# Attention on one NeuronCore: the shifted-V moves issued by SyncE and GpSimd instead of SyncE and ScalarE

## The chip, the cores and the metric

The kernel runs on one core of one Trainium2 chip. Its engines are TensorE (PE; its weight loads are shown apart as PEld), VectorE (DVE), ScalarE (ACT), GpSimd (POOL) and SyncE (SP). SP, ACT and POOL can each issue DMA transfers; all transfers of the core run on the same 16 DMA engines. The metric is the time of one execution on the device in microseconds. Runs of this kernel before the change took 480.32, 483.03 and 484.62 us, median 483.03.

## What is computed

A sequence of 2048 tokens with 512 channels passes through four layers: state-space convolution, attention, convolution, attention, each with a layer norm before it and a residual around it. The change concerns the attention, which looks at eight earlier tokens with a step of two:

```python
def _B_ref(x, wqkv, wo):
    H = 32; Dh = D // H              # D = 512, so Dh = 16
    W, dil = 8, 2
    qkv = ...                        # x @ wqkv, as (3, B, H, S, Dh)
    q, k, v = qkv[0], qkv[1], qkv[2]
    idx = arange(S)[:, None] - (arange(W) * dil)[None, :]
    mask = idx >= 0
    idx_c = where(mask, idx, 0).reshape(-1)
    kg = k[:, :, idx_c, :].reshape(B, H, S, W, Dh)
    vg = v[:, :, idx_c, :].reshape(B, H, S, W, Dh)
    logits = einsum("bhsd,bhswd->bhsw", q, kg) * Dh ** -0.5
    attn = softmax(where(mask, logits, -1e9), axis=-1)
    o = einsum("bhsw,bhswd->bhsd", attn, vg)
    return o.transpose(...).reshape(B, S, D) @ wo
```

## The kernel before

**Stages.** First the convolution's kernel is generated (about 117 us), then come the convolution layer, attention layer 0 (from about 180 to 300 us), the second convolution and attention layer 1 (from about 355 us to the end). Token 16 p + j lies in partition p, column j, so a step of two tokens is a step of two columns, and a step past column 0 goes to the partition above.

**Attention** (`b_layer`). A layer is split into blocks, named in the lists `ORDERS` (line 691): `K0`..`K3` and `Q00`..`Q31` are the projections of keys and queries (line 843 on PE, cast by ACT at 845); `L..` the logits (products `prodqk` on DVE at 871, summed over a head by PE at 885, cast by ACT at 888 into `Lsb`); `S..` the softmax (maxima on DVE at 943, 949 and 951; subtraction on PE at 961 and 962 in layer 0, on DVE at 954 in layer 1; exponentials on ACT at 964 or 955; the sum on PE at 969, its reciprocal by two ACT instructions at 971 and 972, into `sm_rdb`; the scaling on DVE at 973); `V0` and `V1` the two halves of V; `P..` the products with V (`prodpv` on DVE at 992, summed by PE at 999, cast by ACT at 1011); `R..` the output rows (lines 1022 to 1036) and, in layer 0, the norm and the first stage of the next convolution.

**V and its shifted copy.** Each half of V (`fp` 0 or 1, 256 channels) lies in a table `V2` of 128 partitions x 2 x 22 rows x 256. PE projects it in eight pieces (line 899) and ACT casts them into rows 14 to 21 (line 906). The rows below, 0 to 13, hold the same values shifted by one partition or by 64; `v_shift` (line 911) fills them with nine DMA transfers inside SBUF, each of which waits for all eight casts. The first four fill rows 6 to 13 (64, 48, 15 and 1 partitions with 8 KB each, the last with 4 KB), the other five rows 0 to 5 (48, 15, 48 and 15 partitions with 6 KB each, and two with 3 KB). Every product of a half waits for all nine.

**Who issues them.** In half 0 moves 1, 4 and 7 go through ACT's queue and the other six through SP's, in half 1 all nine through SP's. The transfer is issued by the engine in its own sequence, between its other instructions:

```python
act = fp == 0 and k % 3 == 1
o = plan.add("ACT" if act else "SP", 0.65, lambda move=move, act=act: move(nc.scalar if act else nc.sync), need)
```

**What sets the order.** `Plan` (line 621) is a list scheduler that runs while the kernel is built. Each operation has an engine, a cost in us, the operations that it follows and the buffers that it takes. `Plan.run` repeatedly picks the operation that could start earliest by these costs and emits it, a tie going to the lower priority number and then to the order of blocks in `ORDERS`. The emission order is the order in which each engine works, whatever the durations on the chip are. A move costs 0.65 us on its issuing engine; its transfer is an operation of a made-up engine `dma`, which takes one transfer after another at 230 GB/s, and a product may follow 2 us after that. ACT's clock in the plan thus holds three times 0.65 us per layer for moves.

**Other users of the queues.** SP's queue also carries the loads `Kt` of the convolution (line 262; those for the second convolution stand behind V1's moves of layer 0), the zeros of the `V2` tables (737 and 738) and two of the four output stores (142). ACT issues the other two stores. POOL loads five small constants at the start and sets small tables; its last instructions of the kernel's work are at 117 us.

Of the kernel before, what the change touches and what calls it, by code (L numbers as in the profile page):

```python
# [11 lines left out]
ACT = mybir.ActivationFunctionType  # L12
# [694 lines left out]
def b_layer(nc, tc, C, Xg, Ng, Wt, last_layer, y_rows, es_y):  # L707
# [5 lines left out]
    with ExitStack() as es:  # L713
# [43 lines left out]
                m.Z = pool("a_z", 1, es_z).tile([128, NGR, 128], BF, name="Z")  # L757

        pr = PRIO[last_layer]
        plan = Plan({"-": 0.0, "PE": 0.0, "DVE": 0.5, "ACT": 0.5, "SP": 0.0} | {"dma": 0.0})  # L760
        y_sums, x_sums = ((),) * 4, ((0, 1, 2, 3), (0, 1, 2, 3), (0, 1), ())
        PA, PL, PO, PQ, PV = ("psA", 4), ("psL", 2), ("psO", 2), ("prodqk", 5), ("prodpv", 8)
        got = {}
# [147 lines left out]
        def v_shift(fp):  # L911

            moves = [(64, 0, 64, 6, 14, 8, 0), (1, 64, 48, 6, 14, 8, 0), (49, 112, 15, 6, 14, 8, 0), (0, 127, 1, 6, 14, 8, 1)]
            moves += [(64 * h + d, 64 * h + d - 1, n, 0, 16, 6, 0) for h in range(2) for d, n in ((1, 48), (49, 15))]
            moves += [(0, 63, 2, 0, 16, 6, 1)]
            need = [got["V", fp, c, jp] for c in range(2) for jp in range(4)]
            for k, (d, f, n, rd, rs, nr, wrap) in enumerate(moves):
                def move(eng, d=d, f=f, n=n, rd=rd, rs=rs, nr=nr, wrap=wrap):
                    T = m.V2[fp]
                    step = 64 if n == 2 else 1  # L920
                    lanes = [slice(x, x + (n - 1) * step + 1, step) for x in (d, f)]
                    cd, cs = (slice(1, 2), slice(0, 1)) if wrap else (slice(0, 2), slice(0, 2))
                    eng.dma_start(T[lanes[0], cd, rd:rd + nr, :], T[lanes[1], cs, rs:rs + nr, :])
                act = fp == 0 and k % 3 == 1
                o = plan.add("ACT" if act else "SP", 0.65, lambda move=move, act=act: move(nc.scalar if act else nc.sync), need)
                o = plan.add("dma", V_MOVE_US + n * nr * 1e-3 * 512 * (1 if wrap else 2) / V_RATE, lambda: None, [o])
                got["V2", fp].append(plan.add("-", 0.0, lambda: None, [o]))
                got["V2", fp][-1]["lag"] = V_LAND
# [163 lines left out]
        def v_half(fp):  # L1092
            for c in range(2):
                for jp in range(4):
                    proj_v(fp, c, jp)
            v_shift(fp)
# [36 lines left out]
def kernel(  # L1133
# [62 lines left out]
    for layer in range(2):  # L1196
        y_rows, es_y = a_layer(nc, tc, C, Xg, Ng, kt_dram, load_w, Z, es_z)
        Z, es_z = b_layer(nc, tc, C, Xg, Ng, Wt, layer == 1, y_rows, es_y)
# [31 lines left out]
```

## Time and profile before

| | |
|---|---|
| median of three runs | 483.03 us |
| the profiled execution: its own time | 480.45 us |
| the profiled execution: span from first to last instruction | 478.7 us |
| mean granted clock of TensorE | 0.949 |
| DMA packets, data moved | 37873, 45.55 MB |
| DMA data through SP's queue / ACT's queue / POOL's queue | 41.77 / 2.91 / 0.13 MB |
| moves of V: SP issues, duration of one (min, median, max) | 30; 0.559, 0.910, 2.767 us |
| moves of V: ACT issues, duration of one (min, median, max) | 6; 0.677, 1.680, 2.551 us |
| from issue to landing of a move (min, median, max) | 5.8, 7.6, 9.1 us |

The profile is one execution. Busy time of an engine is time in its instructions; an issue of a DMA is not counted as busy and is shown on a queue (SPq, ACTq), with the time for which it holds the engine's sequence. A line of the timeline gives start, duration, engine, line of the code, operation, tiles and, in brackets, how long the engine had been idle before and what ended that; "issue" there means that nothing the profile shows was waited for. The chain of waits is followed back from the last instruction to whatever released each step.

The moves were issued at 221.8 to 229.2 us (layer 0, V0), 244.3 to 254.6 (layer 0, V1), 410.1 to 418.6 (layer 1, V0) and 426.4 to 436.3 (layer 1, V1); the landings recorded last came at 234.2, 257.0, 422.1 and 440.3 us.

### The profile page before, as it was taken

The numbers are of one execution on the slowest core, as the hardware profiler recorded it, in microseconds if no ns is written. First come the engines' busy times: TensorE is split into PE (matmuls) and PEld (weight loads), VectorE is DVE, ScalarE is ACT, GpSimd is POOL, SyncE is SP. The second block draws the span as 40 slices with busy tenths as digits, with TensorE's granted clock in tenths as the row PEclk, the third lists the DMA queues.
The fourth block names the chain that finished last, engine by engine and source line by source line (L and its number), as shares of the span: only waits on it lengthen the run. The fifth ranks groups of instructions, "written<-read, shape, count | busy, mean of one in ns | idle before, by whom it ended". The sixth has DMA issues, their size and how long they took to land.

```text
span 478.7 us, 11624 instructions
## 1 busy us (share of the span) xinstructions
PE 400.8 (84%) x4764; PEld 263.1 (55%) x4764; DVE 411.1 (86%) x848; ACT 334.4 (70%) x568; POOL 5.7 (1%) x26
## 2 busy tenths in 40 slices
PE   2006788979998979999898899879989999888996
PEld 1002358456446754577676665357744567776662
DVE  4899999998349878879899999989878899899990
ACT  5987997974667977854675269969978657652354
POOL 3000000001000000000000000000000000000000
PEclk9999995979999999999999699999999999996699
DMA  8930001424669990003444105029700000645022
GB/s 253 423 117 0 2 0 17 92 56 88 162 155 265 260 286 11 2 2 79 78 94 107 46 1 178 1 60 269 202 1 2 2 3 1 122 91 98 1 88 90
DMA packets 37873, 45.55 MB, mean 95 GB/s; under 512 B 27924, under 2 KB 29204, under 8 KB 36924
## 3 DMA queue, kind: packets, MB, share of 16 engines
q1 hardware_dynamic: 34898, 41.77, 32.8%
q10 hardware_dynamic: 2762, 2.91, 2.6%
q8 instruction: 37, 0.61, 0.5%
q0 software_dynamic: 160, 0.13, 0.1%
q14 instruction: 16, 0.13, 0.1%
HBM read 30.55 MB, written 6.29 MB: 77 GB/s over the span
## 4 chain that ended last, share of the span: by engine, by line
PE 55%; ACT 16%; DVE 15%; DMA 5%; issue 4%; SPq 3%; ACTq 1%; DVEq 0%
PE ps_qk L843 9%; PE ps_v L899 6%; PE po L999 5%; PE psg L453 5%; PE ps_o L1024 4%; PE Lp L885 3%; ACT n_junk L173 3%; ACT xc L289 3%; DVE prodqk L871 3%; DMA Kt<-kt_scratch 3%; PE psk L430 3%; DVE prodpv L992 2%; PE xp L212 2%; ACT Vtab L477 2%; PE vp L279 2%
## 5 line engine op out<-in xcount | busy, mean ns | idle before, releaser
L871 DVE TENSOR_TENSOR prodqk<-qT,N 128x1024 bf16<-128x1024 bf16 (+3 forms) x176 | 83.9, 539 | 4.4 <-ACT N L845 2.2
L992 DVE TENSOR_TENSOR prodpv<-V,Lsb 128x1024 bf16<-128x1024 bf16 (+1 forms) x160 | 81.9, 577 | 1.3 <-DMA V<-V 0.7
L843 PE MATMUL ps_qk<-xnT,wqk 128*128 128x512 bf16 x256 | 61.1, 379 | 2.7 <-ACT xnT L830 2.2
L999 PE MATMUL po<-halves,prodpv 128*128 128x64 bf16 x1024 | 51.5, 208 | 5.3 <-DVE prodpv L992 2.9
L999 PEld LDWEIGHTS <-prodpv 128*128 128x128 bf16 x1024 | 43.1, 107 | 16.9 <-DVE prodpv L992 10.5
L475 PE MATMUL psadd<-cp,sb_ident 128*128 128x512 bf16 (+3 forms) x48 | 18.4, 384 | 33.0 <-DVE cp L334 30.2
L296 DVE TENSOR_TENSOR pab<-xc,Kt 128x2048 bf16<-128x2048 bf16 x32 | 39.1, 1223 | 7.0 <-ACT xc L289 3.6
L453 PE MATMUL psg<-G,rows 128*128 128x512 bf16 x160 | 38.8, 399 | 1.3 <-DMA rows<-KT 1.3
L1011 ACT CAST oT<-po 128x512 bf16<-128x512 f32 x32 | 17.5, 588 | 30.4 <-PE po L999 30.3
L843 PEld LDWEIGHTS <-wqk 128*128 128x128 bf16 x256 | 23.3, 97 | 25.3 <-issue 1.1
L289 ACT CAST xc<-xp 128x1024 bf16<-128x1024 f32 x32 | 32.7, 1021 | 5.7 <-PE xp L212 5.7
L281 ACT CAST VT<-vp 128x1024 bf16<-128x1024 f32 x32 | 32.5, 1020 | 4.4 <-PE vp L279 4.4
L279 PE MATMUL vp<-sb_IC,pab 128*128 128x128 bf16 x512 | 33.7, 219 | 2.1 <-DVE pab L296 2.1
L334 DVE TENSOR_TENSOR cp<-Vtab,L 128x896 bf16<-128x896 bf16 (+6 forms) x64 | 34.1, 594 | 0.7 <-PE psadd L476 0.4
L885 PEld LDWEIGHTS <-prodqk 128*128 128x128 bf16 x1024 | 30.6, 96 | 5.8 <-DVE prodqk L871 1.6
L279 PEld LDWEIGHTS <-pab 128*128 128x128 bf16 x512 | 29.9, 98 | 3.6 <-DVE pab L296 2.6
L885 PE MATMUL Lp<-sb_bones,prodqk 128*128 128x8 bf16 x1024 | 31.0, 166 | 1.0 <-DVE prodqk L871 0.9
L899 PE MATMUL ps_v<-wv,xnT 128*128 128x256 bf16 x256 | 31.4, 272 | 0.5 <-ACT qT L845 0.5
L334 DVE TENSOR_TENSOR cp<-Utab,L 128x256 bf16<-128x256 bf16 (+4 forms) x60 | 29.2, 544 | 0.9 <-PE psadd L476 0.8
L797 DVE BATCH_NORM_STATS2 ln_stats<-X 128x6 f32<-128x512 bf16 x38 | 24.3, 679 | 4.9 <-ACT X L1071 4.6
L430 PE MATMUL psk<-Utab,Vtab 128*64 128x42 bf16 x512 | 24.1, 203 | 4.9 <-ACT KT L438 2.8
L453 PEld LDWEIGHTS <-rows 128*128 128x128 bf16 x160 | 16.1, 102 | 21.8 <-issue 3.8
(160 smaller groups left out, 765.7 us busy)
## 6 DMA issues: line engine op xcount, KB each, us to landing
Kt<-kt_scratch SPq DMA_DIRECT2D x64, 256.0 KB, 5.1
G<-c_G SPq DMA_DIRECT2D x4, 1280.0 KB, 16.6
kt_scratch<-ks SPq DMA_DIRECT2D x16, 256.0 KB, 2.6
X<-in_A_u_dram SPq DMA_DIRECT2D x4, 512.0 KB
F1Tsb<-c_F1T SPq DMA_DIRECT2D x2, 1024.0 KB, 8.5
V<-V SPq DMA_DIRECT2D x4, 512.0 KB
V<-V SPq DMA_DIRECT2D x6, 288.0 KB
F1sb<-c_F SPq DMA_DIRECT2D x1, 1024.0 KB
```

The lines of the kernel that those rows point to most:

```text
L279: nc.tensor.matmul(vp[:, g, :], pab[:, g, ab, :], IC[:, ab, :], start=(ab == 0), stop=(ab == 1))
L289: nc.scalar.copy(xc[:].rearrange("q g o l -> q (g o l)"), xp)
L296: last = nc.vector.tensor_tensor(pab[:], xc[:].to_broadcast([128, 8, 2, 128]), kts[cg][:], ALU.mult)
L334: nc.vector.tensor_tensor(prod[i, r].rearrange("n (h e t) -> n h e t", h=hn, t=2), a(r), m[:, i].unsqueeze(2).to_broadcast([128, hn, e, 2] ...
L430: nc.tensor.matmul(ps[:, hl, 0:2 * NU], V[:, h, r, :, :].rearrange("n v t -> n (v t)"), U[:, h, r, 0:NU, :].rearrange("n u t -> n (u t)"), ...
L453: mms = [nc.tensor.matmul(ps[:, hf, :], rows[:, t, :], Gt[b][:, t, hf * 512:(hf + 1) * 512], start=(t == 0), stop=(t == 4)) for t in range ...
L843: nc.tensor.matmul(t.ps[:], wqk[:, ct, f0:f0 + 128], x_group(g)[:, :, ct], start=(ct == 0), stop=(ct == 3))
L871: nc.vector.tensor_tensor(b.pr[:, u:u + 2 * n, 1 - a, :], cols(qT[i][:, ja * 128:(ja + n) * 128]), cols(kT[i][:, k0:k0 + n * 128]), ALU.mult)
L885: nc.tensor.matmul(t.Lp[:, w, u % 2, u // 2, :], b.pr[:, u].rearrange("f a q -> f (a q)"), bones[:], start=False, stop=(w == W // 2 - 1 an ...
L899: nc.tensor.matmul(t.ps[:, jj, :], tokens(ct, jp * 2 + jj, c), wv[:, ct, fp * 256:(fp + 1) * 256], start=(jj + ct == 0), stop=(jj == 1 and ...
L992: nc.vector.tensor_tensor(t.p2[:, 0:nj, :].rearrange("p j (d h) -> p j d h", d=DH), m.V2[i // 2][:, c, r0:r0 + nj, f0:f0 + 128].rearrange( ...
L999: nc.tensor.matmul(po[jj // k][:, jj % k, c, :], t.p2[:, jj, :], fold, start=(c == 0 and w == 0 and jj % k == 0), stop=(c == 1 and w == W ...
```

## The change

Every second move (1, 3, 5 and 7) is issued by POOL, the others (0, 2, 4, 6 and 8) by SP, in both halves of both layers. ACT issues none. The planner gets a clock for POOL and charges it 0.65 us for each of its moves. Nothing is changed in what is transferred, or in what waits for it.

```diff
@@ -757,7 +757,7 @@
         pr = PRIO[last_layer]
-        plan = Plan({"-": 0.0, "PE": 0.0, "DVE": 0.5, "ACT": 0.5, "SP": 0.0} | {"dma": 0.0})
+        plan = Plan({"-": 0.0, "PE": 0.0, "DVE": 0.5, "ACT": 0.5, "SP": 0.0, "POOL": 0.0, "dma": 0.0})
@@ -921,8 +921,8 @@
                     eng.dma_start(T[lanes[0], cd, rd:rd + nr, :], T[lanes[1], cs, rs:rs + nr, :])
-                act = fp == 0 and k % 3 == 1
-                o = plan.add("ACT" if act else "SP", 0.65, lambda move=move, act=act: move(nc.scalar if act else nc.sync), need)
+                second = k % 2 == 1
+                o = plan.add("POOL" if second else "SP", 0.65, lambda move=move, second=second: move(nc.gpsimd if second else nc.sync), need)
                 o = plan.add("dma", V_MOVE_US + n * nr * 1e-3 * 512 * (1 if wrap else 2) / V_RATE, lambda: None, [o])
```

## The prediction

> **What bounds the kernel.** I read the busy times first, then the busy time in stretches around the four groups of moves (V0 and V1 in each attention layer), then the chain of waits and the timelines there.
>
> ```profile
> PE 400.8 (84%) x4764; PEld 263.1 (55%) x4764; DVE 411.1 (86%) x848; ACT 334.4 (70%) x568; POOL 5.7 (1%) x26
> ...
> 222.00:228.00 6.00, 6.00 (x102) 3.97 (x99) 4.35 (x10) 2.16 (x6) 0.00 (x0) 1.00 0.82 173
> 228.00:236.00 8.00, 6.48 (x58) 4.37 (x57) 6.48 (x15) 6.24 (x13) 0.00 (x0) 1.00 0.57 102
> 236.00:250.00 14.00, 14.00 (x250) 11.19 (x247) 14.00 (x27) 9.06 (x19) 0.00 (x0) 1.00 0.33 67
> ...
> 410.00:416.00 6.00, 5.37 (x124) 4.14 (x122) 4.85 (x14) 2.82 (x7) 0.00 (x0) 1.00 0.78 155
> 416.00:426.00 10.00, 9.39 (x137) 8.54 (x137) 9.71 (x23) 7.99 (x20) 0.00 (x0) 1.00 0.49 94
> 426.00:436.00 10.00, 7.96 (x152) 6.19 (x149) 10.00 (x19) 3.02 (x6) 0.00 (x0) 0.83 0.77 152
> ```
>
> After the stretch come PE, PEld, DVE, ACT and POOL busy, the clock, the DMA share and GB/s. VectorE (DVE) and TensorE (PE) bound the attention together: right behind V0's moves of the first layer both are busy 14.00 of 14.00 us. Only where the moves run is either idle, with the DMA engines near 0.8 busy. What the change can win lies in that idle time. ScalarE's (ACT's) timeline there, first layer:
>
> ```profile
> 222.52 0.68 ACTq L923 DMA_DIRECT2D V<-V  x1
> 222.66 0.61 ACT L888 CAST Lsb<-Lp 128x512 bf16<-128x512 f32 x1
> 223.77 0.37 ACT L971 ACTIVATE den<-den 128x256 f32<-128x256 f32 x1 [0.51 <-PE den L969]
> 223.78 1.33 ACTq L923 DMA_DIRECT2D V<-V  x1
> 225.24 0.39 ACT L972 ACTIVATE sm_rdb<-den 128x256 bf16<-128x256 f32 x1 [1.10 <-issue]
> 225.26 2.55 ACTq L923 DMA_DIRECT2D V<-V  x1
> 227.86 1.07 ACT L845 CAST qT<-ps_qk 128x512 bf16<-128x512 f32 x2 [2.23 <-issue]
> ...
> 229.45 0.43 DVE L943 TENSOR_TENSOR sm_m<-Lsb 128x512 bf16<-128x512 bf16 x1 [3.11 <-ACT Lsb L888]
> ```
>
> Three issues hold ACT's queue for 4.56 us; two casts behind the third start 2.23 us late, the logits' cast (line 888) behind them is late too, and DVE waits 3.11 us for it. Last, the chain of waits at V1 of the second layer:
>
> ```profile
> 425.80 0.59 ACT V L906
> ...
> 427.11 2.32 SPq L923
> ...
> 434.83 5.47 DMA V<-V
> ...
> 440.43 0.70 DVE prodpv L992
> ```
>
> All nine moves go through SyncE (SP) from 426.41; the last data land at 440.30, 13.9 us after the evict, and DVE waits 0.67 us.
>
> **The change part by part.** Over both layers ACT's moves go from 6 to 0, SP's from 30 to 20, GpSimd's (POOL's) from 0 to 16. In V0, moves 1 and 7 go from ACT to POOL, 3 and 5 from SP to POOL, 4 from ACT to SP; in V1, moves 1, 3, 5, 7 from SP to POOL. No byte is saved: each half still moves 1782 KB (127 lanes x 8 KB, 126 lanes x 6 KB, two wraps).
>
> *Moves off ACT, first layer.* ACT gains 4.56 us, but that is not the gain of the kernel. DVE has work until 226.35, so its wait shrinks by at most the 3.1 us from there to 229.45. Behind it come 6 us of DVE work, then the first prodpv at 235.52, which needs V0; V0's last landing in the trace is at 234.16. So DVE can come forward only 1.36 us before it waits for the moves instead. PE is idle 1.52 us in 228 to 236 and full before and behind, which allows about the same. Gain: 1.4 us, if V0 lands when it does now.
>
> *Moves off ACT, second layer.* The issues hold ACT 5.15 us; the reciprocal (sm_rdb) waits 1.22 us behind the last, and DVE 1.28 us for it. V0 lands at 422.08, the first prodpv starts at 423.42: slack 1.34. PE has 0.63 + 0.61 us idle from 410 to 426. Gain: 1.2 us.
>
> *Moves off SP.* V0, on two queues now, lands 12.3 and 12.0 us after the first issue; V1, on one, 12.6 (244.34 to 256.96) and 13.9. A second queue thus buys 0 to 1.9 us, because the transfers fill most of it: 1782 KB in 10.5 us is 170 GB/s. I take 12.3 for all four halves. V1 of the second layer then lands 1.6 us earlier and its 0.67 us wait goes. V1 of the first is first read by DVE at 262.4, covered by 5.4 us. Behind SP's V1 moves there stand the next layer's Kt loads, from 254.66; they may start some 4 us earlier and share the DMA engines with V1's tail, inside that cover. In the second layer only the output stores at 457 stand behind. Nothing for that.
>
> *Moves onto POOL.* POOL has nothing between 118 and 478 us, so no one is queued behind its four moves and their wait for V's evicts. The trace has five small POOL loads, from the start:
>
> ```profile
> Drow<-in_A_Dskip_dram POOLq DMA_DIRECT2D x1, 1.0 KB, 4.6
> ...
> sb_IC<-c_IC POOLq DMA_DIRECT2D x1, 64.0 KB, 4.1
> ...
> rows<-KT SPq DMA_DIRECT2D x24, 20.0 KB, 1.9
> ```
>
> One issue takes 0.51 to 0.68 us, 128 rows included; a half's four take 2.0 to 2.7 us. A landing is 2.7 us later than SP's small ones (4.6 against 1.9). The wait on POOL is the four moves one after the other, 2.7 + 4.6 = 7.3 us plus their 568 KB beside SP's 1214 KB; with the engines shared evenly that is 2 x 568 / 170 = 6.7 us, so they are down by about 10 of the 12.3 us. SP's last move still ends the half: I take no change, with bounds of -2 (the engines at the 16 x 4096 B / 319 ns = 205 GB/s that the median packet gives) and +5 us (rival A).
>
> *DVE beside POOL.* The windows of the moves hold only TENSOR_TENSOR on DVE. No descriptor writing overlaps DVE in the trace. Bounds: 0, and 16 x 0.53 = 8.5 us if each issue stops a DVE that is full. The nearest row is POOL's 128x512 memset at 116.45: 0.53 us beside DVE's TENSOR_SCALARs, 0.55 us alone. I take 0.
>
> The Trainium skill ("SBUF — State Buffer", section "SBUF: two separate sides") speaks against the change: GpSimd writes a DMA's descriptors through a port pair shared with VectorE, and a VectorE instruction in a two-port mode shuts it out. Its section "Who interferes with whom" exempts tensor_tensor, which it says, as inferred, takes only the read side. No run here shows either. By the page's 3.1 us for a shut-out DMA, four make 12.4 us and V would land at 17.0 us instead of 12.3; as an estimate that costs 3 x 4.7 - 3.3 = 11 us.
>
> *The planner's order.* The planner charged ACT 0.65 us for each of three moves per layer and now charges nothing, so instructions are emitted in another order behind V0. PE is full there, and what ACT does next waits for PE, so I expect few swaps. Nearest price of a bad one: DVE's 1.69 us wait for sm_rdb at 286.3. Bounds -2 to +3; I take 0.4 per layer, 0.8 in all.
>
> *Sum.* -1.4 - 1.2 - 0.7 + 0.8 = -2.5 us. The profiled execution took 480.45 us (span 478.7 plus 1.75 around it), so 478.0 for such a one; the median of the three runs is 2.6 us higher, so 483.0 - 2.5 = 480.5.
>
> **Rivals.**
>
> *A, slower: POOL writes descriptors only while DVE is idle.* It decides once the fourth issue ends later than 12.3 - 4.6 = 7.7 us behind the evict, that is at 1.9 us an issue instead of 0.53. A half needs 4 x 0.53 = 2.1 us of DVE idle. First layer, V0: the 3.1 us gap gives it, nothing lost. Second layer, V0: only 1.3 us are there; DVE reaches prodpv at 422.1, stands still, POOL does the remaining 0.8 us and the data land 4.6 us later, 427.5 against 423.4: +4.1. V1: DVE has no gap before 439.8, so 2.1 + 4.6 puts prodpv at 446.5 against 440.4: +6.1. With -1.4 and the order's 0.8: +9.6, 492.6. If instead POOL stops DVE, 8.5 - 2.5 = +6.0, 489.0. For it: DVE is 97 to 100% busy at these places, and no DMA of POOL has run beside it. Against it: the memset. The skill's exemption stands against it too.
>
> *B, order:* another sequence behind V0 makes new waits of 1.7 us, two per layer: 4 x 1.7 - 3.3 = +3.5, 486.5; or it packs DVE better: DVE's idle time from the first issue to the last landing of all four halves is 51.1 - 45.85 = 5.3 us, and with the 1.69 us at 286.3 gone as well the time is 476.0 at best. For it: every wait behind V0 hangs on this order. Against: PE full.
>
> *C, no gain:* V lands later by about what ACT gives back (x = 1.1 us at three places): 483. For it: POOL's landings of 4.6 us. It differs from the forecast by less than can be measured.
>
> **How the numbers follow.** Forecast 0.40, C 0.15, A 0.23, B slower 0.12, B faster 0.10. The forecast's own range is 477.5 to 483.5. About 1% (4.8 us) is what a measurement of this kernel can tell from no change; its three runs span 4.3. Faster than 478.2: B faster and a little of the forecast, 0.15. Slower than 487.9: A and a tail of B, 0.28. Within: 0.57. The range leaves out A's far end and the last of B faster: 476 to 490.
>
> **What would show it.** Right: no ACT gap "<-issue" behind V0; line 943's wait gone or turned into prodpv waiting about 1.7 us for V in the first layer; POOL's L923 rows near 0.5 us; V landing 12 us behind its evict everywhere. Wrong: POOL rows of 2 us or more, prodpv waiting for V several us at 422 or 440 (A); DVE's prodqk of 128x1024 above 0.69 us (DVE stopped by POOL); or waits on lines other than these behind V0 (B).

## The result, and the profile after

The changed kernel took 478.79 us (median of 21 runs, 476.10 to 481.92) beside 481.37 us before it (21 runs, 478.81 to 485.61): ratio 0.9948, 95% interval 0.9927 to 0.9968, that is -2.5 us. The same kernel, timed again in a later set, gave 477.61 us beside 481.67 us, ratio 0.9918 (0.9895 to 0.9940). It is a little faster, by 0.5 and 0.8 per cent in the two sets. The forecast gain of 2.5 us came in the first set, and about 4.0 us came in the second. The forecast time of 480.5 us was 1.7 us too high: it was counted from a median of three runs, 483.0 us, where 21 runs put the kernel before at 481.4.

The two profiled spans hide this: 478.4 us after, 478.7 before. The attention simply starts later in the profile of after. The zeros of its first `V2` table, which the change does not touch, are written at 192.23 us instead of 190.16; over the profiles of this study that moment lies anywhere between 188.6 and 193.2 us. From 160 to 190 us the mean granted clock was 1.00 in the profile of before and 0.94 in that of after; whether this is the whole shift is not shown. So each layer is read from its own first move; over the two stretches compared here the granted clock is 0.93 and 0.87 in both profiles. From there to the layer's last `prodpv` the first layer takes 74.77 us instead of 76.23, and from there to the last cast of `X` the second takes 63.23 us instead of 64.62: together -2.85 us.

The busy times, and the windows around the moves (those of the first layer put 2 us later than before's), with PE, PEld, DVE, ACT and POOL busy, the clock, the DMA share and GB/s:

```profile
PE 396.1 (83%) x4728; PEld 260.3 (54%) x4764; DVE 410.6 (86%) x848; ACT 334.8 (70%) x568; POOL 14.6 (3%) x42
```

```profile
224.00:230.00 6.00, 6.00 (x103) 4.05 (x102) 4.91 (x12) 4.24 (x9) 2.22 (x4) 1.00 0.86 198
230.00:238.00 8.00, 7.95 (x127) 6.24 (x127) 7.97 (x17) 5.66 (x11) 0.00 (x0) 1.00 0.48 85
238.00:252.00 14.00, 14.00 (x206) 10.48 (x203) 14.00 (x27) 9.26 (x19) 2.23 (x4) 1.00 0.46 95
...
410.00:416.00 6.00, 6.00 (x139) 4.93 (x137) 6.00 (x18) 4.88 (x11) 2.23 (x4) 1.00 0.70 168
416.00:426.00 10.00, 9.47 (x169) 8.68 (x168) 9.44 (x22) 6.66 (x13) 0.35 (x1) 1.00 0.51 88
426.00:436.00 10.00, 7.86 (x129) 6.42 (x126) 10.00 (x21) 3.16 (x7) 1.88 (x4) 0.62 0.93 183
```

POOL's 14.6 us and 42 instructions include its 16 issues, which the profile counts as busy, unlike those of SP and ACT. In the first two windows DVE was busy 4.35 + 6.48 us of 14; now it is 4.91 + 7.97, and PE has no hole left (6.00 + 7.95). At 410 DVE is full where it had lost 1.15 us. POOL's four issues for V1 of the first layer and those for V0 of the second lie inside windows in which DVE and PE are both full (238 to 252, 410 to 416); in the window of V0 of the first layer DVE is busy 4.91 of 6 us. ACT's timeline behind V0 of the first layer:

```profile
223.76 1.09 ACT L964 ACTIVATE Lsb<-ps_sub 128x512 bf16<-128x512 f32 x2
224.73 0.61 ACT L888 CAST Lsb<-Lp 128x512 bf16<-128x512 f32 x1
225.41 0.58 ACT L845 CAST qT<-ps_qk 128x512 bf16<-128x512 f32 x1
225.90 0.37 ACT L971 ACTIVATE den<-den 128x256 f32<-128x256 f32 x1
226.30 0.38 ACT L972 ACTIVATE sm_rdb<-den 128x256 bf16<-128x256 f32 x1
226.81 0.58 ACT L845 CAST qT<-ps_qk 128x512 bf16<-128x512 f32 x1
```

No issue and no bracket with "<-issue" is left; the 1.10 and 2.23 us gaps are gone, and the instructions follow one another. DVE's timeline, first layer and then second:

```profile
229.50 0.63 DVE L871 TENSOR_TENSOR prodqk<-qT,N 128x512 bf16<-128x512 bf16 x2 [1.09 <-ACT N L845]
230.04 0.42 DVE L943 TENSOR_TENSOR sm_m<-Lsb 128x512 bf16<-128x512 bf16 x1
...
235.59 1.90 DVE L992 TENSOR_TENSOR prodpv<-V,Lsb 128x1024 bf16<-128x1024 bf16 x3
...
422.19 0.69 DVE L992 TENSOR_TENSOR prodpv<-V,Lsb 128x1024 bf16<-128x1024 bf16 x1
423.44 1.29 DVE L992 TENSOR_TENSOR prodpv<-V,Lsb 128x1024 bf16<-128x1024 bf16 x2 [0.56 <-DMA V<-V]
...
439.02 4.91 DVE L992 TENSOR_TENSOR prodpv<-V,Lsb 128x1024 bf16<-128x1024 bf16 x8
```

In the first layer line 943's wait of 3.11 us has become one of 1.09 us, for another cast of ACT that PE's projections hold up. In the second layer the wait of 0.67 us for V1 (at 440) is gone, and a wait of 0.56 us for V0 has come in its place at 423. The chain of waits runs through V0's moves there, where it ran through V1's before:

```profile
410.10 0.59 ACT V L906
410.71 0.66 SPq L923
411.37 0.05 issue
411.42 2.87 SPq L923
...
415.32 8.00 DMA V<-V
...
423.44 1.29 DVE prodpv L992 x2
```

POOL's timeline, with the idle time before each group, and the groups of line 923 (duration in ns, min/median/max; first and last start):

```profile
224.16 2.22 POOL L923 DMA_DIRECT2D V<-V  x4 [105.08 <-ACT V L906]
244.78 2.23 POOL L923 DMA_DIRECT2D V<-V  x4 [18.40 <-ACT V L906]
410.98 2.23 POOL L923 DMA_DIRECT2D V<-V  x4 [163.97 <-DVE Lsb L954]
```

```profile
L923 SPq DMA_DIRECT2D V<-V x20: 655/1192/2867, 223.9 to 430.8; - x20
...
L923 POOL DMA_DIRECT2D V<-V x16: 497/574/587, 224.2 to 427.3; - x16
```

POOL takes 0.50 to 0.59 us for an issue, all four right behind the evict. The halves are down 11.7, 12.0, 12.6 and 11.9 us behind their first issue (12.3, 12.6, 12.0 and 13.9 before).

### The profile page after: what moved, and what is told of

Same layout as the page of the kernel before. It is cut to its first block, busy times and chain, and to the rows that moved or that the text cites. A ratio compares the mean times of both kernels' runs of the same rounds, so it can differ in the third digit from the quotient of the medians.

```text
span 478.4 us, 11628 instructions
## 1 busy us (share of the span) xinstructions
PE 396.1 (83%) x4728; PEld 260.3 (54%) x4764; DVE 410.6 (86%) x848; ACT 334.8 (70%) x568; POOL 14.6 (3%) x42
## 4 chain that ended last, share of the span: by engine, by line
PE 55%; DVE 17%; ACT 17%; issue 4%; DMA 3%; SPq 2%; ACTq 0%; DVEq 0%
PE ps_qk L843 9%; PE psg L453 6%; DVE prodpv L992 6%; PE po L999 5%; PE ps_o L1024 5%; ACT xc L289 4%; PE pt L200 3%; PE Lp L885 3%; PE ps_v L899 3%; DVE prodqk L871 3%; ACT n_junk L173 3%; PE vp L279 3%; PE xp L212 3%; PE psk L430 2%; ACT Vtab L477 2%
## 5 line engine op out<-in xcount | busy, mean ns | idle before, releaser
L453 PE MATMUL psg<-G,rows 128*128 128x512 bf16 x156 | 40.1, 414 | 5.0 <-DMA klast<-KT 4.5
L845 ACT CAST N<-ps_qk 128x512 bf16<-128x512 f32 x32 | 18.8, 586 | 14.2 <-PE ps_qk L843 14.1
```

The costliest lines, as they stand in the source:

```text
L453: mms = [nc.tensor.matmul(ps[:, hf, :], rows[:, t, :], Gt[b][:, t, hf * 512:(hf + 1) * 512], start=(t == 0), stop=(t == 4)) for t in range ...
```

## The experiments

Two things change at once: the queues, and the planner's charges, from which the order of the instructions follows. The theory: the gain is ACT rid of its six issues; which queue takes them, and the new order, are worth little. Rivals: the second queue brings it (V down earlier), POOL's descriptor writing costs DVE or waits for it, or the order decides. All versions but the probe differ in the two lines of the change alone. The first diff is against the changed kernel, and those behind it show only what stands in place of its two added lines. Where one of them shows the queue alone, the line with the planner's charge is that of the first version for the new order and that of the second for the old order.

**The new order with the old queues.** The planner charges POOL and SP, while ACT and SP issue as before.

```diff
-                second = k % 2 == 1
-                o = plan.add("POOL" if second else "SP", 0.65, lambda move=move, second=second: move(nc.gpsimd if second else nc.sync), need)
+                queue = nc.scalar if fp == 0 and k % 3 == 1 else nc.sync
+                o = plan.add("POOL" if k % 2 else "SP", 0.65, lambda move=move, queue=queue: move(queue), need)
```

> PE and DVE run in the changed kernel's order, but the moves go through the queues of before (ACT issues 1, 4 and 7 of V0). Queue theory (the gain is ACT's and SP's queue time): no gain, between 0 and +1 us of 481.4, and ACT again shows idle time ended by 'issue' behind V0; since ACT's three issues now stand close together they may hold it 4 to 6 us in one piece. Order theory (the gain comes from the new order): -2.6 us, the same as the changed kernel.

Measured: 486.51 us, ratio 1.0112 (1.0065 to 1.0160), +5.2 us: a miss of the theory, which priced the order by itself. ACT's timeline of this version, first layer and then second:

```profile
222.35 3.08 ACTq L923 DMA_DIRECT2D V<-V  x1
222.77 0.38 ACT L971 ACTIVATE den<-den 128x256 f32<-128x256 f32 x1
225.55 0.38 ACT L972 ACTIVATE sm_rdb<-den 128x256 bf16<-128x256 f32 x1 [2.40 <-issue]
...
411.84 3.19 ACTq L923 DMA_DIRECT2D V<-V  x1
```

A planner that does not know of ACT's issues packs ACT's work as if that time were free, and single issues hold ACT for 3.08 and 3.19 us. The first `prodpv` comes 15.2 us behind the first move in both layers, against 11.7 and 11.5 in the changed kernel with the same order. So the issues on ACT cost more than the 2.0 us that the change gave back at that place, and the old charges had hidden a part of them.

**The new queues with the old order.**

```diff
+                queue = nc.gpsimd if k % 2 else nc.sync
+                o = plan.add("ACT" if fp == 0 and k % 3 == 1 else "SP", 0.65, lambda move=move, queue=queue: move(queue), need)
```

> PE, DVE and the rest of ACT run in the order of before; the moves go through SP and POOL as changed. Queue theory: -2.6 to -3.3 us (the forecast's -1.4 - 1.2 - 0.7, with or without its 0.8 for the order). In layer 0 the 3.1 us wait of line 943 falls by about 2 us or more, in layer 1 the 1.3 us wait for sm_rdb and the 0.67 us wait for V1 go. Order theory: 0 us.

Measured: 477.93 us, ratio 0.9939 (0.9912 to 0.9965). The whole gain is there without the new order.

**All nine moves on SP, new order, then old order.** ACT is free, and there is no second queue.

```diff
+                queue = nc.sync
```

> The changed kernel's order, all 36 moves on SP. If freeing ACT is what counts and POOL does not: the same -2.6 us as the changed kernel. If the second queue counts too: V0 lands 12.6 to 13.9 us after its first issue instead of 11.7 to 12.6, so prodpv waits 1 to 1.5 us for V0 in each layer, V1 of layer 1 is waited for again, and the time is -1.0 us (0 to -2).

> PE and DVE in the order of before, all 36 moves on SP: the one difference from before is that ACT no longer issues its six moves. If freeing ACT is the whole gain: -2.9 us of 481.4, as with SP and POOL in this order (477.9). If POOL's share counts in this order: prodpv waits for V in layer 1 and the gain is 1.5 us or less.

Measured: 478.72 us, ratio 0.9955 (0.9933 to 0.9976), and with the old order 479.36 us, ratio 0.9961 (0.9942 to 0.9981). Both gain nearly as much as the change, without GpSimd. In the first of them the halves land 13.2 to 13.3 us behind their first issue, 0.6 to 1.7 us later than in the changed kernel; with the old order they land at 12.6 to 13.5. DVE's timeline of the first shows what that costs, first layer and then second:

```profile
235.44 1.89 DVE L992 TENSOR_TENSOR prodpv<-V,Lsb 128x1024 bf16<-128x1024 bf16 x3
...
423.94 1.29 DVE L992 TENSOR_TENSOR prodpv<-V,Lsb 128x1024 bf16<-128x1024 bf16 x2 [1.18 <-DMA V<-V]
```

In the first layer `prodpv` starts at 235.44 with no wait, although moves 4 to 7 land from 234.2 to 237.08: its first block reads only the rows that moves 0 to 3 fill, and these were down by 232.82. (On the chip, then, a product waits for the moves whose rows it reads; that it follows all nine is true of the planner's order alone.) In the second layer the second product needs a later move and waits 1.18 us. With the old order it waits 1.17; in the four profiles of the versions with the queues of the change it waits 0, 0.37, 0.56 and 0.85 us. The second queue thus shows in the traces with 0.3 to 1.2 us at one place and is lost in the medians' intervals.

**All nine moves on POOL, new order, then old order.** Nine issues in place of four beside a busy DVE.

```diff
+                queue = nc.gpsimd
```

> All 36 moves on POOL, the changed kernel's order. Theory (the 16 DMA engines set the landing, whichever queue feeds them, and POOL writes descriptors at its own pace beside DVE): nine issues of 0.50 to 0.60 us, V landed 12 to 13 us behind its first issue, 478.8 us within 1. Rival A (POOL shut out or shutting DVE out): issues of 1 us or more, or prodqk of 128x1024 above 0.70 us, and 483 us or more.

> Old order, all nine moves of every half on POOL. ACT-freed theory: as the version before, 0.993 to 0.995, since neither the second queue nor POOL itself is worth anything measurable; V landed 12 to 13 us after its first issue. Rival (POOL's issues cost a busy DVE): 36 issues of 0.5 us, up to 18 us, at the least some us slower than the version with 16.

Measured: 479.18 us, ratio 0.9961 (0.9932 to 0.9989), and with the old order 477.89 us, ratio 0.9925 (0.9906 to 0.9944). The groups of line 923 in the version with the new order:

```profile
L923 POOL DMA_DIRECT2D V<-V x36: 524/593/616, 220.5 to 426.7; - x36
```

No issue took over 0.62 us, and the halves landed 12.1 to 13.0 us behind the first. DVE's `prodqk` of 128x1024 took 687 ns on average here, against 684 in the kernel before. With the old order the halves landed at 12.2 to 14.6 us, two of the four later than the 12 to 13 expected. POOL's and DVE's timelines there, second layer:

```profile
413.30 0.57 POOL L923 DMA_DIRECT2D V<-V  x1 [1.01 <-DMA V<-V]
...
421.47 1.29 DVE L992 TENSOR_TENSOR prodpv<-V,Lsb 128x1024 bf16<-128x1024 bf16 x2 [1.59 <-DMA V<-V]
```

The move that POOL issued late at 413.30 landed last, at 421.25, and `prodpv` waited 1.59 us for it. That is one wait of this size in eight halves; the time of this version shows no loss by it. Had each issue stopped DVE for its 0.53 us, the 20 more of them would put these versions some 10.6 us above the one with 16; they are level with it.

**V1 alone as in the change, V0 as before.**

```diff
+                queue = (nc.gpsimd if k % 2 else nc.sync) if fp else (nc.scalar if k % 3 == 1 else nc.sync)
+                o = plan.add(("POOL" if k % 2 else "SP") if fp else ("ACT" if k % 3 == 1 else "SP"), 0.65, lambda move=move, queue=queue: move(queue), need)
```

> Only the second half of V goes through SP and POOL; V0 keeps ACT's three issues, and the order is that of before. Forecast's third term alone: V1 of layer 1 lands 11.9 us instead of 13.9 us after its first issue, the 0.67 us wait of prodpv goes, -0.7 us; ACT's idle time ended by 'issue' stays at 3.3 us in layer 0 and 1.2 us in layer 1. If V1 were hidden anyway: 0 us.

Measured: 480.60 us, ratio 0.9999 (0.9972 to 1.0027). Nothing is gained where ACT keeps its issues; line 943's wait is back with 3.4 us. `prodpv` no longer waits for V1 in the second layer, where it landed 11.5 us behind its first issue, so the wait went as expected. The 0.7 us that this should save lie inside the interval of the time, so they are neither shown nor excluded.

**Every second move on ACT in place of POOL.** 16 issues on ACT, with the planner not charged for them.

```diff
+                queue = nc.scalar if k % 2 else nc.sync
+                o = plan.add("POOL" if k % 2 else "SP", 0.65, lambda move=move, queue=queue: move(queue), need)
```

> The changed kernel with ACT in POOL's place: moves 1, 3, 5 and 7 of every half on ACT, 16 in all, in the new order. Theory (an issue holds ACT while the transfers before it drain, and the new order leaves ACT no room for that): at least the 486.5 us of the kernel with six, up to 490. If a second queue of any kind were as good: 478.8.

Measured: 493.62 us, ratio 1.0277 (1.0227 to 1.0328), +12.3 us, at the same order and with the same split as the change. The groups of line 923 and DVE's longest wait behind V0 of the first layer:

```profile
L923 ACTq DMA_DIRECT2D V<-V x16: 673/1205/3122, 223.8 to 447.2; - x16
```

```profile
DVE Lsb L973 <- ACT sm_rdb L972: 3.3, 1, 3.3
```

The same moves cost their engine 0.57 us each on POOL and 1.2 us on ACT (medians; up to 3.1 on ACT), where the reciprocals and casts behind it are waited for.

**POOL's issues beside another form of DVE's work.** In the changed kernel, four extra stores of a normed tile to DRAM are issued by POOL while DVE does the first norm's TENSOR_SCALARs; the output is the same.

```diff
             first_norm_apply(nc, C["n1"], Xg, Ng)
+        probe = nc.dram_tensor("probe", (4, 128, D), BF)
+        for j in range(4):
+            nc.gpsimd.dma_start(probe.ap()[j], Ng[0][:, j, :])
```

> The changed kernel, and in addition POOL stores four 128 KB rows of the first norm's output into a scratch tensor, each as soon as DVE has written it, while DVE goes on with the 15 TENSOR_SCALARs of that norm (112 to 117 us). Measures the disputed cost by itself beside another instruction of DVE. If only TENSOR_TENSOR spares POOL: POOL's issues there take 1 us or more instead of 0.50 to 0.59, or DVE's TENSOR_SCALARs more than 0.44 us. If DVE and POOL do not meet at all: both as before.

DVE's and POOL's timelines there, from its one profile, and DVE's group with its mean in ns:

```profile
111.50 5.26 DVE L192 TENSOR_SCALAR N<-X,n_rstd,n_nb 128x512 bf16<-128x512 bf16 x16
```

```profile
112.21 2.41 POOL L1193 DMA_DIRECT2D probe<-N  x4 [106.64 <-DVE N L192]
```

```profile
L192 DVE TENSOR_SCALAR N<-X,n_rstd,n_nb 128x512 bf16<-128x512 bf16 x16 | 5.3, 410 | 0.0
```

The four issues took 0.55 to 0.66 us in the middle of sixteen unbroken TENSOR_SCALARs, which took 410 ns each against 405 in the changed kernel without them. Neither held up the other.

The same form of DVE's work does lose time to another instruction of POOL. In the profile of before, one of the same sixteen TENSOR_SCALARs started at 116.28, beside POOL's memset of 116.45, and took 848 ns (min/median/max):

```profile
L192 DVE TENSOR_SCALAR N<-X,n_rstd,n_nb x16: 405/409/848, 111.4 to 116.3; 128x512 bf16<-128x512 bf16 x16
```

In the two other profiles in which the memset overlaps one of them, the longest took 837 and 845 ns; in the ten in which it does not, none took over 418 ns. So a POOL memset and this form do meet, and four DMA issues of POOL did not.

**The order once more**, with the change itself and its old-order twin in one set.

> The change as it is, timed once more beside the two versions with the old order. Both theories: 0.995 of the kernel before, about 479 us, T00 to the first prodpv 11.7 us and 11.5 us in the second layer.

> Old order, queues of the change. Theory that the new order costs time: last prodpv of the second layer 42.7 us after its first instead of 43.6, last X cast 7.8 us behind it instead of 8.2, so 0.8 to 1.2 us below the change in the same call (ratio to the kernel before about 0.993). Rival: both orders pack alike, the difference of 0.4 us in the medians so far was noise, 0.995 again.

Measured: the change 0.9918 (0.9895 to 0.9940), the old order 0.9907 (0.9874 to 0.9939). The two are level within their intervals, as in the first set (0.9948 and 0.9939).

The stages of all versions side by side, in us, one profile each (first move to first `prodpv`; first move to the last `prodpv` in layer 0 and to the last cast of `X` in layer 1):

| version | order | to first prodpv, layer 0 / 1 | to the end, layer 0 / 1 | sum | ratio of times |
|---|---|---|---|---|---|
| before | old | 13.70 / 13.30 | 76.23 / 64.62 | 140.85 | 1 |
| the change | new | 11.70 / 11.48 | 74.77 / 63.23 | 138.00 | 0.9948 |
| the change again | new | 11.70 / 11.49 | 74.25 / 63.52 | 137.77 | 0.9918 |
| same queues | old | 11.75 / 11.72 | 75.48 / 62.29 | 137.77 | 0.9939 |
| same queues, again | old | 11.75 / 11.72 | 74.78 / 62.74 | 137.52 | 0.9907 |
| all on SP | new | 11.71 / 11.48 | 74.79 / 63.85 | 138.64 | 0.9955 |
| all on SP | old | 11.76 / 11.72 | 74.61 / 63.55 | 138.16 | 0.9961 |
| all on POOL | new | 11.43 / 11.22 | 74.65 / 62.54 | 137.19 | 0.9961 |
| all on POOL | old | 11.49 / 11.46 | 74.02 / 63.70 | 137.72 | 0.9925 |
| V1 as changed | own | 13.97 / 12.43 | 77.62 / 63.00 | 140.62 | 0.9999 |
| old queues | new | 15.21 / 15.18 | 78.51 / 66.63 | 145.14 | 1.0112 |
| ACT and SP | new | 17.11 / 17.16 | 84.91 / 71.62 | 156.53 | 1.0277 |

Two pairs of rows start from another point. In the two rows with the same queues in the old order, layer 0 is counted from the second move: there move 3, with one partition, was issued 5.02 us ahead of the others, so on the chip that move does not wait for all eight casts. And where all moves are on POOL the first of them starts 0.29 us behind the evict instead of 0.03; with this added in both layers, their sums are 137.7 and 138.2.

The column to the first `prodpv` parts them cleanly: about 11.5 wherever ACT issues nothing, whatever the queue and the order, and 12.4 to 17.2 wherever it does. Twice the same kernel differs by 0.3 to 0.7 us in a layer's whole, so the eight rows without ACT, 137.5 to 138.6 counted from the evict, cannot be ranked; none of them beats the change by more than the runs can tell.

## Why the prediction was right, and where its steps were not

**Moves off ACT, first layer (-1.4 forecast).** The mechanism was right: the issues' gaps are gone, and DVE comes forward. The bound was wrong. It was put at V0's last landing, 1.36 us ahead of the first `prodpv`; but that product reads only the rows of moves 0 to 3, which in the profile of before were down by 233.09, so it had 2.4 us. It came forward by 2.0 us. What DVE still waits for ahead of it is ACT's cast into `N` at line 845 (1.09 us), which waits for PE. By the layer's end 1.46 us of the 2.0 are left in the profiled pair. The term's size thus came out right on a wrong bound, which is luck.

**Moves off ACT, second layer, and V1 (-1.2 and -0.7).** The first `prodpv` came forward by 1.8 us, more than the 1.2 allowed, for the same reason. The bound holds for the second product, which does need later moves: it started 13.9 us behind the first move before and 12.7 after. V1's wait of 0.67 us went as forecast, but a wait of 0.56 us for V0 took its place, which the prediction had not named. The layer gained 1.39 us of the 1.9 in this pair of profiles. V1's term by itself was not confirmed.

**Moves off SP and onto POOL (no change).** The outcome was right. All four halves lie at 11.7 to 12.6 us where 12.3 was taken, and an issue of POOL takes 0.50 to 0.59 us (0.51 to 0.68 taken). POOL's moves were down 8.7 to 10.9 us behind the first issue, where about 10 was given; but the prediction's own two terms, 7.3 and 6.7 us one behind the other, add up to 14.0. Issues and transfers overlapped, so this number was right without its working. SP's queue alone lands V at 12.6 to 13.5 us over both orders. In the new order a second queue buys 0.6 to 1.7 us of landing, inside the 0 to 1.9 given, and next to no time. The Trainium skill ("DMA: Bandwidth & Descriptors", section "Issuing engines are not separate DMA queues") says the same: several issuing engines save only the time on the sequencers that start the transfers. These runs agree on the transfers (138.0 us with two queues, 138.6 with one); the sequencer time, which it calls usually small beside the transfer, was here the whole gain.

**DVE beside POOL (0), and rival A.** The term was right, and is now shown and not only argued: 36 issues at 0.52 to 0.62 us beside a full DVE, no wait of several us for V (the longest is 1.59), and times level with the version with 16. The reason that the prediction gave was not sound. It read the memset's row for POOL's half alone, 0.53 us; the TENSOR_SCALAR beside that memset took 848 ns instead of 409, so the row spoke for rival A's second form, in which POOL stops DVE. DMA issues did not do what the memset did. The exemption of tensor_tensor that the Trainium skill states ("SBUF — State Buffer", section "Who interferes with whom") agrees with the 36 issues here. Beside TENSOR_SCALARs four issues showed nothing either; longer instructions of DVE and other forms were not tried.

**The planner's order (+0.8, few swaps).** Laid side by side, the two orders differ in few places in the first layer, 4 instructions of DVE, and in more in the second, about 21 of DVE; ACT has some 15 over both. They cost nothing that the runs resolve: new against old order 0.9948 and 0.9939, 0.9918 and 0.9907, 0.9955 and 0.9961, 0.9961 and 0.9925. Nothing measured supports the +0.8, and rival B fell with it. The other three terms, -3.3 us together, stand against -2.85 and -3.08 us in the two pairs of profiles and against -2.5 and -4.0 us in the two sets of runs. That the sum of four terms met the first set's -2.5 us to the tenth is in part luck. What the step left out is that charge and issue belong together: the new charges with the old issues cost 5.2 us.

**Rival C** (no gain) falls: both intervals of the ratio lie below 1.

## What to carry to other kernels

Move DMA issues off an engine whose next instructions are waited for; which idle queue takes them matters far less, and a second queue shortened a batch of transfers little here, by 0.6 to 1.7 of 13 us. Read the bound of a wait from the rows that the waiting instruction reads, not from the last landing of the whole tile. And where a scheduler holds a charge for the issuing engine, change charge and queue together: issues on ACT that it did not know of cost 5 us (six of them) to 12 us (sixteen) here.

## What was not expected of the hardware

The price of an issue depends on the engine that makes it. The same moves took 0.49 to 0.62 us each on POOL in every version, while on SP they took 0.56 to 3.50 us and on ACT 0.67 to 3.19 us, the long ones while earlier moves of the burst were in flight. With all nine on POOL, POOL itself had to wait before an issue at some places, as the waits of the old-order version show (total us, times, longest):

```profile
POOL V L923 <- DMA V<-V: 1.8, 2, 1.0
```

Each time it is the ninth move, and it starts 0.28 us after the first move of its half has landed. By the operands in the trace, the moves on POOL use eight semaphores in turn, so the ninth takes that of the first again, and it is this landing that POOL waited for (0.8 to 1.0 us, where the first landed late). One of these two late moves is the one that `prodpv` waited for above. Nine transfers through POOL alone landed 12.1 to 14.6 us behind the first issue, through SP alone 12.6 to 13.5, though POOL's small loads at the start had taken 2.7 us longer than SP's.
